# Attention with sink heads, then a soft mixture of experts: one weight loaded in 18 pieces, a fixed order behind the last load, a re-drawn plan

## The chip, the cores and the metric

The kernel runs on one core of a Trainium2 chip. A core has TensorE (PE, matmuls; its weight loads are shown as PEld), VectorE (DVE), ScalarE (ACT), GpSimd (POOL) and SyncE (SP), each with its own instruction queue, and 16 DMA engines that all queues share. The metric is the device time of one execution in microseconds (us), the median of several runs.

## What is computed

```
q, k, v: 4 batches, 8 heads, 768 positions, 64 per head (float32)
scores = q k^T / 8, causal; a head that is not a "retrieval" head sees only
         the first 4 positions and the last 64
x      = softmax(scores) v, as a matrix of 3072 rows by 512
logits = x phi                       (phi: 512 x 32 = 8 experts x 4 slots)
slots  = softmax over the rows(logits)^T x           (32 x 512)
out_e  = relu(slots_e w1[e]) w2[e]   (w1: 512 x 1024, w2: 1024 x 512, 8 experts)
result = softmax over the slots(logits) out          (3072 x 512)
```

All inputs are float32 in memory: q, k and v together 18.9 MB, w1 and w2 together 33.6 MB. The loads convert them to bfloat16 on the way.

## The kernel before

**Stages.** The attention runs in 16 steps (`p = 4*b + n`: batch b, head pair n). Per batch, q, k and v are loaded raw (`load_raw`, 768 KB each as it lands), turned by TensorE (`Tq`, `Tk`, `Tv`, line 513), and copied out (`Eq`, `Ek`, `Ev`). Per step there are score matmuls (`QK`, line 538), exponentials on ScalarE (`EX`, line 609), masks on VectorE (`MK`, line 555), the product with v (`PV`, line 669), the norm (`NM`, line 683) and the turning of the result (`XT`, `XE`). Per batch, the logits and the slots are gathered (`LG`, `EL`, `DS`, `SA`, `TE`, `EE`). When the last batch is through, the experts run for all 32 slots: `SI`, `H` (first matmul), `HR` (relu), `TH`/`HE` (turning), `W2.0` to `W2.7` (second matmul, line 882).

**The loads.** 29 large loads are issued from GpSimd by `dma`/`load_w`/`load_raw` (line 281): q, k, v of four batches, the eight first weights w0 to w7 and the eight second weights w8 to w15. 11 buffers of 8 KB per partition (`slot`, class S8) hold raw inputs and weights in turn; the last weights go into memory that attention has left (`late_mem`). The last weight, w15, comes in two loads: w15a holds 5 of its 8 parts (`FL = 5`), w15b the other 3. w5 is one load of 2 MB (1 MB as it lands), 128 rows of 4096 values.

**Behind the last load.** `SOa` (line 891, ScalarE) scales what the weights up to w15a have made. The first 512 result rows (group 0, four tiles r = 0 to 3, the first of them in two halves) do not wait for the rest: `OM.0.r` multiplies them with SOa's result, and `OG.0.r` adds the part of w15b by three matmuls with operands `gT`, prepared beforehand by `GP.x` (line 911) and `GE.x`. Meanwhile `W2b` (three matmuls with w15b's parts) and `SOb` (line 891, ScalarE: "the late scaling") make the complete slot output, from which all further tiles are multiplied (`OM.1.0.0` and on, line 935). Each tile is scaled and copied out (`OE`, lines 951 on ScalarE and 953 on VectorE) and stored by SyncE (`ST`, line 964) in ten stores.

**The order.** The order of every engine's instructions is not written out: `Plan.run` simulates the engines with estimated durations, picks at each step the operation that can start first (within 0.12 us, by the lowest key), and the kernel emits the operations in that order. Each engine then runs its queue strictly in order, with semaphore waits. `SHIFT` adds an offset to the key of named operations, `ALT` fixes the engine of others; both are long tables of drawn numbers. `FETCH` is the estimated time that TensorE needs for the next block of 128 instructions. In `dma`, an operation `issue` costs 0.62 on GpSimd in the plan, and its `emit` calls one `dma_start`. The plan has buffers for PSUM: classes SC (2), TR (2) and PV (1).

**Zeros.** Where the plan sees TensorE idle in the tail up to the last weight, matmuls with zeros (line 1034) fill the time.

Of the kernel before, what the change touches and what calls it, by code (L numbers as in the profile page):

```python
# [15 lines left out]
ACT = mybir.ActivationFunctionType  # L16
# [3 lines left out]


SHIFT = {
    "phi cast": 1.5, "phi": 6.5, "Tv0.1": 3.5, "Tv0.3": 8, "Tq1.0": -0.5, "Tq1.2": 2, "Tk1.1": 8, "Tk1.2": -1,
    "Tk1.3": 4, "Tv1.1": 3, "Ek2.1": -3.5, "Tk2.2": 3.5, "Tk2.3": 2, "Tv2.0": 8, "Eq3.0": 1, "Tq3.1": 5.5,
    "Tq3.3": 1, "Tk3.0": 8, "Tk3.2": -3.5, "Tv3.0": 3.5, "Ev3.1": -7, "QK.1.3": 3, "QK.1.4": 3, "MK.1.2": 4.5,
    "QK.2.0": -2, "QK.2.1": 2.5, "QK.2.2": 8, "QK.2.3": -5.5, "QK.2.4": -2.5, "VB.3": -6.5, "QK.3.2": 7.5,
    "MK.3.1": 8, "QK.3.4": 4.5, "QX.0.2": 8, "MK.4.0": -3, "QK.4.2": 4.5, "EX.4.3": -6.5, "QK.4.4": 4.5,
    "QK.5.0": -2.5, "QK.5.1": -1, "QK.5.2": 1.5, "QK.5.4": -1.5, "QK.6.3": -2, "QK.6.4": 3, "MK.6.2": 2.5,
    "EX.7.0": -7.5, "EX.7.3": -7, "MK.7.1": -4, "QK.8.0": -8, "QK.8.2": -7.5, "QK.8.4": -8, "VB.9": -5,
    "QK.9.2": -2, "MK.9.2": 4.5, "V2.10": 4, "QK.10.3": 4, "MK.10.1": 5, "V2.11": -1, "QK.11.0": 1.5,  # L30
    "QK.11.1": 1.5, "QK.11.3": 8, "MK.11.2": -7, "QX.2.0": -4.5, "V2.12": 8, "QK.12.0": -6, "QK.12.1": 3,
    "MK.12.1": 4, "QK.13.2": 0.5, "QK.13.3": -2.5, "MK.13.1": -4.5, "V2.14": -2, "QK.14.2": -1.5, "MK.14.2": -8,
    "QK.15.0": -2.5, "XE.0": 2.5, "PV.2.0": 6.5, "PV.3.0": 4.5, "PV.4.3": 8, "PV.5.0": 4, "PV.7.4": -2,
    "PV.7.5": -3.5, "DS.1": 3, "PV.8.0": 4.5, "PV.8.5": 4, "XT.9": 7.5, "XT.10": 7, "XT.12": 5, "PV.13.1": 5,
    "PV.13.5": 7.5, "XT.13": 8, "PV.15.0": -2, "H.1.0": -8,
}
ALT = {
    "Ev0.3": 0, "Eq1.1": 0, "Ek1.2": 1, "Ek1.3": 0, "Ev1.2": 0, "Eq2.1": 0, "Eq2.3": 0, "Ek2.0": 0, "Ek3.1": 1,
    "Ek3.3": 0, "Ev3.0": 0, "VB.7": 0, "VB.13": 0, "EE.1": 0, "EE.2": 0, "XE.14": 0, "HR.1.0": 1,
}  # L40


# [12 lines left out]
class Plan:  # L55
# [3 lines left out]
    OVERLAP = {"ACT": 0.10, "DVE": 0.085, "GEN": 1.45}  # L59
    SWITCH, BONUS, ACTPEN = 0.13, 4.0, 0.4  # L60

    CHUNK, FIRST, FETCH = 128, 97, 5.5

    def __init__(self, classes):
        self.ops, self.free = [], {c: [(0.0, s) for s in range(n)] for c, n in classes.items()}
# [107 lines left out]
def kernel(  # L173
# [13 lines left out]
    nc = tc.nc  # L187
    P = 128
    B, H, S, D = q.shape
# [26 lines left out]
    phi = sb.tile([P, 4, NS], BF16, name="phi")  # L216
# [29 lines left out]
    scb = [ps.tile([P, 2, 512], F32, name=f"sc{i}") for i in range(2)]  # L246
    trb = [ps.tile([P, 512], F32, name=f"tr{i}") for i in range(2)]
    pvb = ps.tile([P, 2, 512], F32, name="pv")

    def tr_bf(s, n):  # L250
# [9 lines left out]
    NGT, FL = 4, 5  # L260
    gT = mk[:, 3200:3200 + 128 * NGT * (8 - FL)].rearrange("p (f c) -> p f c", c=128 * NGT)
    slot_out_a = mk[:, 4736:5248]
    hg = mk[96:128, 5248:5248 + 128 * (8 - FL)].rearrange("p (f c) -> p f c", c=128)
# [3 lines left out]
    pl = Plan({"S8": 11, "QT": 2, "KT": 2, "VT": 1, "VB": 2, "VF": 3, "PT": 2, "PTX": 2, "XB": 2,  # L267
               "XT": 1, "SC": 2, "TR": 2, "PV": 1})
# [3 lines left out]
    def copy(o, dst, src):  # L272
        if o.eng == "ACT":
            nc.scalar.copy(dst, src)
        else:
            nc.vector.tensor_copy(dst, src)  # L276


    def dma(name, key, nbytes, ndesc, buf, dst, src, deps=()):
        iss = pl.op("issue " + name, {"POOL": 0.62}, key, deps=deps, acq=[buf] if buf else [], lead=1.3,  # L280
                    emit=lambda o: nc.gpsimd.dma_start(dst(), src))  # L281
        issues.append(iss)
        gen = pl.op("gen " + name, {"GEN": 1.45}, key, deps=[iss])
        return pl.op("land " + name, {"DMA": dma_us(nbytes, ndesc)}, key, deps=[gen], lead=3.3)
# [22 lines left out]
    wland = [None] * NW  # L307
    late_mem, last_lands = {}, []

    def w_view(i):  # L310
        m = late_mem[i]() if i in late_mem else slots[wbuf[i].slot][:, :]
        return m.rearrange("p (a f) -> p a f", a=4 if i < NE else 8)

    def load_w(i, key, deps=()):
        if i < NE:
            src = moe_w1[i].rearrange("(di do) f -> di do f", do=4)
        else:
            src = moe_w2[i - NE].rearrange("(fi fo) d -> fi fo d", fo=8)
            if i == NW - 1:
                for k, (f0, f1) in enumerate(((0, FL), (FL, 8))):  # L320
                    last_lands.append(dma(f"w15{'ab'[k]}", key + 0.1 * k, (f1 - f0) << 18, 128, None,
                                          lambda f0=f0, f1=f1: w_view(i)[:, f0:f1, :], src[:, f0:f1, :], deps=deps))
                wland[i] = last_lands[0]
                return
        wland[i] = dma(f"w{i}", key, 2 << 20, 128, None if i in late_mem else wbuf[i],
                       lambda: w_view(i), src, deps=deps)


    def tables(o):
# [232 lines left out]
    for b in range(B):  # L562
        for n in range(4):
            p = 4 * b + n
# [79 lines left out]
    for b in range(B):  # L644
        for n in range(4):
            p = 4 * b + n
# [242 lines left out]
    def emit_so(o, d=None):  # L889
        if o.eng == "ACT":  # L890
            nc.scalar.activation(d, pvb[:, 0, :], ACT.Copy, scale=rcs[:, 0:1])
        else:
# [1 line left out]

    so_a = pl.op("SOa", {"ACT": 0.69, "DVE": 0.74}, kt + 20, deps=[w2o[-1], o_rc], need=[so],
                 emit=lambda o: emit_so(o, slot_out_a))
    w2b = pl.op("W2b", {"PE": 0.3}, kt + 25.25, n=8 - FL, deps=[so_a, last_lands[1]], need=[so],
                emit=lambda o: emit_w2(o, fos=tuple(range(FL, 8))))
    so_b = pl.op("SOb", {"ACT": 0.69}, kt + 29.0, deps=[w2b], rel=[so], emit=lambda o: emit_so(o, slot_out))

# [4 lines left out]
    o_hg = pl.op("HG", {"DVE": 0.4}, kt + 8, deps=hse[1] + [o_rc], emit=emit_hg)  # L905
    ge = []
    for x in range(8 - FL):
        gb = Buf("TR")

        def emit_gp(o, x=x, gb=gb):  # L910
            nc.tensor.matmul(trb[gb.slot][:, 0:128 * NGT].rearrange("p (r c) -> p r c", r=NGT), hg[:, x, :],
                             expT[96:128, 0:NGT, 0:128], start=True, stop=True, tile_position=(96, 0))

        a = pl.op(f"GP.{x}", {"PE": 0.25}, kt + 8, n=1, deps=[o_hg] + [eto[b] for b in range(B)], acq=[gb], emit=emit_gp)
        ge.append(pl.op(f"GE.{x}", {"DVE": 0.62, "ACT": 0.69}, kt + 8, deps=[a], rel=[gb],
                        emit=lambda o, x=x, gb=gb: copy(o, gT[:, x, :], trb[gb.slot][:, 0:128 * NGT])))


    def ot_view(gi):
# [5 lines left out]
    for m, (gi, r, d0, d1) in enumerate(parts):  # L925
        c = ["SC", "TR", "SC", "TR"][m] if m < 4 else pat[(m - 4) % 5]
        bf = Buf(c)

        def bank(bf=bf, c=c, w=d1 - d0):
            return (trb[bf.slot] if c == "TR" else scb[bf.slot][:, 0, :] if c == "SC" else pvb[:, 0, :])[:, 0:w]  # L930

        early = gi == 0 and r < NGT

        def emit_om(o, gi=gi, r=r, d0=d0, d1=d1, bank=bank, early=early):
            nc.tensor.matmul(bank(), out_lhs(gi, r), (slot_out_a if early else slot_out)[:, d0:d1], start=True, stop=not early)

        def emit_og(o, r=r, d0=d0, d1=d1, bank=bank):
            for x in range(8 - FL):
                nc.tensor.matmul(bank(), gT[:, x, 128 * r:128 * (r + 1)], w_view(NW - 1)[:, FL + x, d0:d1],
                                 start=False, stop=(x == 7 - FL))  # L940

        a = pl.op(f"OM.{gi}.{r}.{d0}", {"PE": 0.22 * (d1 - d0) / 512}, kt + 24 + m, n=1,
                  deps=[so_a] if early else [so_b], acq=[bf], emit=emit_om)
        if early:
            a = pl.op(f"OG.{gi}.{r}.{d0}", {"PE": 0.22 * (8 - FL) * (d1 - d0) / 512}, kt + 29 + 0.1 * m, n=8 - FL,
                      deps=[a, last_lands[1]] + ge, need=[bf], emit=emit_og)

        def emit_oe(o, gi=gi, r=r, d0=d0, d1=d1, bank=bank):
            d, sc_ = ot_view(gi)[:, r, d0:d1], rrow[:, 4 * gi + r:4 * gi + r + 1]
            if o.eng == "ACT":  # L950
                nc.scalar.activation(d, bank(), ACT.Copy, scale=sc_)
            else:
                nc.vector.tensor_scalar(d, bank(), sc_, None, op0=ALU.mult)  # L953

        w = (d1 - d0) / 512
        oe.setdefault((gi, r), []).append(
            pl.op(f"OE.{gi}.{r}.{d0}", {e_: u for e_, u in (("ACT", 0.22 + 0.47 * w), ("DVE", 0.21 + 0.54 * w))
                                        if not early or e_ == ("ACT", "DVE", "DVE", "DVE", "ACT")[m]}, kt + 30 + m, deps=[a, o_rw],
                  rel=[bf], emit=emit_oe))
    store_parts = [(0, r, r + 1) for r in range(4)] + [(1, 0, 2), (1, 2, 4)] + [(gi, 0, 4) for gi in range(2, 6)]  # L960
    for gi, r0, r1 in store_parts:
        def emit_st(o, gi=gi, r0=r0, r1=r1):
            dst = out[512 * gi:512 * (gi + 1), :].rearrange("(p r) d -> p r d", r=4)
            nc.sync.dma_start(dst[:, r0:r1, :], ot_view(gi)[:, r0:r1, :])

        pl.op(f"ST.{gi}.{r0}", {"SP": 0.7}, kt + 40 + 4 * gi + r0, deps=[x for r in range(r0, r1) for x in oe[gi, r]],
              emit=emit_st)

    order = pl.run()
# [107 lines left out]
```

## Time and profile before

| | us |
|---|---|
| median of 3 runs | 154.38 (152.85, 154.87, 154.38) |
| profiled execution | 152.3 |
| its span, first to last instruction | 150.5 |
| granted TensorE clock, mean over the span | 0.978 |

| engine | busy us | share of span |
|---|---|---|
| PE | 130.1 | 86% |
| DVE | 117.0 | 78% |
| ACT | 106.1 | 71% |
| POOL | 18.6 | 12% |

The durations that follow come from that one execution, counted from the span's start. The loads from GpSimd carry 26.22 MB as it lands (52.49 MB read from memory), the stores 6.29 MB.

Some single events that the text refers to: q3 is issued at 38.05 and its sixteen completion records (one for each DMA engine) lie at 69.72 to 72.46; those of w4 end at 62.94, those of w5 lie at 66.04 to 68.91, those of w15a end at 127.79, those of w15b lie at 125.80 to 129.75. The first store is issued at 131.32, the last at 140.26.

In the profile's timeline a line has start, duration, engine, line, operation, output and input, count, and in brackets the idle time of the engine before it with what ended it. In the chain of waits a line has start, duration, engine, output and line. The slices cut the span into 40 equal parts of 3.76 us; a digit is the busy share in tenths.

### The profile page before, as it was taken

The numbers are of one execution on the slowest core, as the hardware profiler recorded it, in microseconds if no ns is written. First come the engines' busy times: TensorE is split into PE (matmuls) and PEld (weight loads), VectorE is DVE, ScalarE is ACT, GpSimd is POOL, SyncE is SP. The second block draws the span as 40 slices with busy tenths as digits, with TensorE's granted clock in tenths as the row PEclk, the third lists the DMA queues.
The fourth block names the chain that finished last, engine by engine and source line by source line (L and its number), as shares of the span: only waits on it lengthen the run. The fifth ranks groups of instructions, "written<-read, shape, count | busy, mean of one in ns | idle before, by whom it ended". The sixth has DMA issues, their size and how long they took to land.

```text
span 150.5 us, 5245 instructions
## 1 busy us (share of the span) xinstructions
PE 130.1 (86%) x2328; PEld 83.4 (55%) x2328; DVE 117.0 (78%) x243; ACT 106.1 (71%) x126; POOL 18.6 (12%) x38
## 2 busy tenths in 40 slices
PE   6999998999989999888999998998899899798000
PEld 2465565676766677584677766765674444332000
DVE  3889489998789999877999898999976970289200
ACT  3083899889899998788999998999903340379100
POOL 6922111110110001101001202010300000000000
PEclk9999999999999999999999999999999999999965
DMA  3999999999999999999999999999999997079993
GB/s 42 198 212 219 219 209 212 218 223 211 214 211 214 222 216 218 211 212 211 217 221 217 218 216 213 218 213 216 216 218 216 216 205 151 7 255 404 429 422 163
DMA packets 6552, 32.90 MB, mean 219 GB/s; under 512 B 642, under 2 KB 770, under 8 KB 4098
## 3 DMA queue, kind: packets, MB, share of 16 engines
q0 software_dynamic: 4944, 26.22, 85.3%
q1 hardware_dynamic: 1440, 6.29, 10.4%
q8 instruction: 18, 0.29, 0.7%
q10 hardware_dynamic: 146, 0.07, 0.2%
q14 instruction: 4, 0.03, 0.1%
HBM read 52.49 MB, written 6.29 MB: 391 GB/s over the span
## 4 chain that ended last, share of the span: by engine, by line
PE 56%; DVE 18%; ACT 13%; issue 5%; DVEq 0%; ACTq 0%
ACT pt L609 12%; PE pv L669 10%; PE sc L538 10%; PE tr L513 8%; PE pv L1034 6%; PE pv L416 3%; PE tr L695 3%; PE pv L882 3%; DVE pt L555 3%; PE tr L572 3%; DVE slot L953 2%; DVE rcs L811 2%; DVE vx L276 2%; DVE xv L683 2%; DVE qk L276 2%
## 5 line engine op out<-in xcount | busy, mean ns | idle before, releaser
L609 ACT ACTIVATE pt<-sc 128x1024 bf16<-128x1024 f32 x80 | 76.7, 1035 | 5.3 <-PE sc L538 4.4
L538 PE MATMUL sc<-qk 64*128 64x512 bf16 (+3 forms) x256 | 30.7, 307 | 1.5 <-ACT pt L609 0.8
L555 DVE TENSOR_TENSOR pt<-pt,msk 128x1024 bf16<-128x1024 bf16 (+1 forms) x48 | 30.4, 640 | 0.7 <-ACT pt L609 0.6
L669 PE MATMUL pv<-vx,pt 128*128 128x65 bf16 x352 | 26.5, 193 | 0.6 <-issue 0.6
L669 PEld LDWEIGHTS <-pt 128*128 128x128 bf16 x640 | 23.7, 97 | 5.7 <-issue 4.4
L513 PEld LDWEIGHTS <-slot 96*64 96x64 bf16 x768 | 18.6, 110 | 7.9 <-issue 6.5
L513 PE MATMUL tr<-ident,slot 96*64 96x96 bf16 x704 | 21.3, 208 | 0.9 <-issue 0.7
L669 PE MATMUL pv<-vf,pt 128*128 128x65 bf16 x288 | 21.2, 194 | 0.0
L683 DVE TENSOR_TENSOR xv<-pv,rs 128x768 bf16<-128x768 f32 x16 | 15.3, 958 | 0.6
L538 PEld LDWEIGHTS <-qk 64*128 64x128 bf16 x256 | 10.5, 94 | 8.6 <-issue 2.8
L276 DVE COPY qk<-tr 128x768 bf16<-128x768 bf16 x23 | 12.3, 550 | 0.0
L281 POOL DMA_DIRECT2D slot<-in_moe_w_dram x11 | 6.1, 559 | 38.2 <-PE tr L513 27.8
L1034 PE MATMUL pv<-zero 128*128 128x512 bf16 (+1 forms) x43 | 10.2, 373 | 0.0
L953 DVE TENSOR_SCALAR slot<-tr,rrow 128x512 f32<-128x512 f32 (+1 forms) x6 | 4.0, 701 | 7.4 <-issue 6.8
L572 PE MATMUL tr<-ident,xv 128*128 128x128 bf16 x96 | 8.1, 220 | 1.7 <-issue 1.7
L276 DVE COPY xv<-tr 128x768 bf16<-128x768 bf16 x14 | 7.4, 551 | 2.6 <-PE tr L513 2.4
L276 DVE COPY vx<-tr 128x768 bf16<-128x768 bf16 x14 | 7.7, 553 | 2.1 <-PE tr L572 2.1
L695 PE MATMUL tr<-ident,xv 128*128 128x128 bf16 x96 | 8.0, 219 | 0.8 <-DVE xv L683 0.5
L276 DVE COPY xT<-tr 128x768 bf16<-128x768 bf16 x14 | 7.7, 552 | 0.9 <-PE tr L695 0.8
L572 PEld LDWEIGHTS <-xv 128*128 128x128 bf16 x96 | 5.6, 97 | 4.1 <-issue 3.7
L1034 PEld LDWEIGHTS <-zero 128*128 128x128 bf16 x59 | 4.9, 97 | 5.3 <-issue 1.1
L695 PEld LDWEIGHTS <-xv 128*128 128x128 bf16 x96 | 5.7, 97 | 3.1 <-issue 1.5
(122 smaller groups left out, 159.3 us busy)
## 6 DMA issues: line engine op xcount, KB each, us to landing
slot<-in_moe_w_dram POOLq DMA_DIRECT2D x11, 1024.0 KB, 23.9
out_dram<-slot SPq DMA_DIRECT2D x4, 1024.0 KB, 7.6
slot<-in_q_dram POOLq DMA_DIRECT2D x4, 768.0 KB, 26.8
slot<-in_k_dram POOLq DMA_DIRECT2D x4, 768.0 KB, 27.9
slot<-in_v_dram POOLq DMA_DIRECT2D x4, 768.0 KB, 23.2
qk<-in_moe_w_dram POOLq DMA_DIRECT2D x1, 1024.0 KB, 18.7
vx<-in_moe_w_dram POOLq DMA_DIRECT2D x1, 1024.0 KB, 21.5
xv<-in_moe_w_dram POOLq DMA_DIRECT2D x1, 1024.0 KB, 20.0
```

The lines of the kernel that those rows point to most:

```text
L276: nc.vector.tensor_copy(dst, src)
L281: emit=lambda o: nc.gpsimd.dma_start(dst(), src))
L513: nc.tensor.transpose(t[64 * i:64 * (i + 1), :, s, :], rv[:, i, 8 * c + s, :], ident[0:96, 0:96])
L538: nc.tensor.matmul(scb[sc.slot][:, i, c:c + 128 * nb], kk, qq.rearrange("p b c -> p (b c)"), start=True, stop=True)
L555: nc.vector.tensor_tensor(pw, pw, mw, op=ALU.mult)
L572: nc.tensor.transpose(t[:, 128 * j:128 * (j + 1)], vT[:, 6 * n + j, :], ident)
L609: nc.scalar.activation(pTs[PTb[b, n].slot][:, :, 512 * g:512 * (g + 1)], scb[sc.slot], ACT.Exp, scale=scale)
L669: nc.tensor.matmul(pvb[:, h, 65 * i:65 * (i + 1)], lt, rhs, start=(j == 0), stop=(j == i))
L683: nc.vector.tensor_tensor(xo, pvw[:, :, :, 0:64], r.rearrange("p i (j o) -> p i j o", o=1).to_broadcast([P, 2, 6, 64]), op=ALU.mult)
L695: nc.tensor.transpose(t[:, 128 * i:128 * (i + 1)], xv[:, i, 128 * n:128 * (n + 1)], ident)
L953: nc.vector.tensor_scalar(d, bank(), sc_, None, op0=ALU.mult)
L1034: nc.tensor.matmul(bank[:, c0:c0 + w], zero[:, 0:128], zero[:, 0:w], start=(c0 == 0), stop=True, skip_group_check=True)
```

## The change

Five things change:

1. `dma` takes a list `cuts`, and issues one `dma_start` for each cut. w5 alone gets such a list, `UNEVEN`, of 18: rows 0 to 111 whole; rows 112 to 127 from value 1024 on; and for n = 0 to 7 the 128 values from 128 n on, once for rows 112 to 126 - n and once for rows 127 - n to 127. The plan's cost of the issue is 0.62 for each piece.
2. `SHIFT` and `ALT` are replaced by other drawn numbers, for all stages; `FETCH` is 6.2 instead of 5.5.
3. Behind w15b, TensorE's order is written out by added dependences: OM of the tiles (0,0) in two halves, (0,1), (0,2), then OG of the same, then W2b, then OM and OG of (0,3), then OM.1.0.0. The plan's cost and key of W2b change.
4. The engines of the first five OE are ACT, DVE, DVE, ACT, DVE instead of ACT, DVE, DVE, DVE, ACT. The third GP/GE pair uses a bank of class SC instead of TR.
5. A store's cost on SyncE in the plan is 0.4 instead of 0.7.

```diff
 SHIFT = {
-    "phi cast": 1.5, "phi": 6.5, "Tv0.1": 3.5, "Tv0.3": 8, "Tq1.0": -0.5, "Tq1.2": 2, "Tk1.1": 8, "Tk1.2": -1,
...
+    "phi cast": 7.5, "P2": 5, "Tk0.2": -2.5, "Tk0.3": -1.5, "Eq1.3": 2, "Ek1.2": 3.5, "Tk1.3": 3.5, "Tv1.1": 8,
...
-    CHUNK, FIRST, FETCH = 128, 97, 5.5
+    CHUNK, FIRST, FETCH = 128, 97, 6.2
...
-    def dma(name, key, nbytes, ndesc, buf, dst, src, deps=()):
-        iss = pl.op("issue " + name, {"POOL": 0.62}, key, deps=deps, acq=[buf] if buf else [], lead=1.3,
-                    emit=lambda o: nc.gpsimd.dma_start(dst(), src))
+    def dma(name, key, nbytes, ndesc, buf, dst, src, deps=(), cuts=()):
+        def emit(o):
+            d = dst()
+            for r, c in cuts or [(slice(None), None)]:
+                if c is None:
+                    nc.gpsimd.dma_start(d[r], src[r])
+                else:
+                    nc.gpsimd.dma_start(d[r].rearrange("p a f -> p (a f)")[:, c],
+                                        src[r].rearrange("p a f -> p (a f)")[:, c])
+
+        iss = pl.op("issue " + name, {"POOL": 0.62 * max(1, len(cuts))}, key, deps=deps, acq=[buf] if buf else [], lead=1.3,
+                    emit=emit)
...
+    UNEVEN = [(slice(0, 112), None), (slice(112, 128), slice(1024, 4096))]
+    for n in range(8):
+        cut = slice(128 * n, 128 * (n + 1))
+        UNEVEN += [(slice(112, 127 - n), cut), (slice(127 - n, 128), cut)]
...
-                       lambda: w_view(i), src, deps=deps)
+                       lambda: w_view(i), src, deps=deps, cuts=UNEVEN if i == 5 else ())
...
-    w2b = pl.op("W2b", {"PE": 0.3}, kt + 25.25, n=8 - FL, deps=[so_a, last_lands[1]], need=[so],
+    w2b = pl.op("W2b", {"PE": 0.55}, kt + 29.0, n=8 - FL, deps=[so_a, last_lands[1]], need=[so],
...
-        gb = Buf("TR")
+        gb = Buf("TR" if x < 2 else "SC")
...
-                                        if not early or e_ == ("ACT", "DVE", "DVE", "DVE", "ACT")[m]}, kt + 30 + m, deps=[a, o_rw],
+                                        if not early or e_ == ("ACT", "DVE", "DVE", "ACT", "DVE")[m]}, kt + 30 + m, deps=[a, o_rw],
...
+    tail = {o.name: o for o in pl.ops}
+    seq = ["OM.0.0.0", "OM.0.0.256", "OM.0.1.0", "OM.0.2.0", "OG.0.0.0", "OG.0.0.256", "OG.0.1.0", "OG.0.2.0", "W2b",
+           "OM.0.3.0", "OG.0.3.0", "OM.1.0.0"]
+    for x, y in zip(seq[:-1], seq[1:]):
+        tail[y].deps.append(tail[x])
+        tail[y].ndep += 1
+        tail[x].succ.append(tail[y])
...
-        pl.op(f"ST.{gi}.{r0}", {"SP": 0.7}, kt + 40 + 4 * gi + r0, deps=[x for r in range(r0, r1) for x in oe[gi, r]],
+        pl.op(f"ST.{gi}.{r0}", {"SP": 0.4}, kt + 40 + 4 * gi + r0, deps=[x for r in range(r0, r1) for x in oe[gi, r]],
```

## The prediction

> **What bounds the kernel now.** I read the page's slices first.
>
> ```profile
> PE   6999998999989999888999998998899899798000
> DMA  3999999999999999999999999999999997079993
> GB/s 42 198 212 219 219 209 212 218 223 211 214 211 214 222 216 218 211 212 211 217 221 217 218 216 213 218 213 216 216 218 216 216 205 151 7 255 404 429 422 163
> ```
>
> The DMA row is at its ceiling from the second slice to the 33rd: the loads run without a hole from 2.80 us (first packet) to 129.75 us, then there is a hole of one slice, then the stores. Next the chain of waits, at the end of the loads.
>
> ```profile
> 123.41 3.21 PE pv L882 x56
> 126.61 1.24 PE pv L1034 x6
> 127.86 0.59 PE pv L882 x5
> 128.47 0.70 ACT msk L891
> ```
>
> The second expert matmul has eaten seven weights by 126.61, fills the time with zeros (L1034) and goes on at 127.86, when w15a has landed: so the loads set the end, and compute is ahead of them by 1.24 us. What follows w15b's landing at 129.75 is a fixed tail of 20.75 us to the span's end at 150.5; the profiled execution took 152.3, so 1.8 lie outside the span. The runs have their median at 154.38 (152.85 to 154.87): the sum below is made on 152.3, and 2.1 us are added for the median.
>
> Third, GpSimd's timeline, the queue that issues every large load.
>
> ```profile
> 7.06 0.58 POOL L281 DMA_DIRECT2D slot<-in_moe_w_dram  x1
> 8.45 0.65 POOL L281 DMA_DIRECT2D slot<-in_moe_w_dram  x1 [0.80 <-DMA slot<-in_q_dram]
> 12.12 0.76 POOL L281 DMA_DIRECT2D slot<-in_q_dram  x1 [3.02 <-DMA slot<-in_k_dram]
> 16.73 0.64 POOL L281 DMA_DIRECT2D slot<-in_k_dram  x1 [3.84 <-DMA slot<-in_v_dram]
> ...
> 33.09 0.53 POOL L281 DMA_DIRECT2D slot<-in_moe_w_dram  x1 [3.33 <-PE tr L513]
> 38.05 0.65 POOL L281 DMA_DIRECT2D slot<-in_q_dram  x1 [4.43 <-DMA slot<-in_moe_w_dram]
> 42.64 0.64 POOL L281 DMA_DIRECT2D slot<-in_k_dram  x1 [3.94 <-PE pv L669]
> ```
>
> The ninth load (w2, at 8.45) goes into a slot nobody has used, and still waits for q0, the first; the tenth waits for k0, the second; the eleventh for v0, the third. The completions fall on eight semaphores in turn, and each issue waits for the load eight before it on the same one (w1, the eighth, lands at 37.47, and q3, the sixteenth, goes out at 38.05). So at most eight GpSimd loads are in flight, whatever their size. With loads of 0.75 to 1 MB that is some 30 us of queue: w5, out at 33.09, lands at 68.91.
>
> **The change, part by part.**
>
> *The triangle.* w5 becomes 18 loads: one of 112 rows, one of 16 rows by 3072 values, and 16 of 128 values by 1 to 15 rows. Call them w5.0 to w5.17; they take 18 places in the eight-deep window, and q3, k3, v3 and all later weights stand behind them on GpSimd. w5.0 to w5.7 replace old loads as these land (the last place comes free with w4's landing, 62.94). w5.8 must wait for w5.0 itself, w5.9 for w5.1, and so on; q3 comes after w5.17. So when w5.0 has landed, nothing of size is queued, and the DMA engines run dry until q3.
>
> When: w5's sixteen completion records lie at 66.04 to 68.91. A weight's packet of 8192 bytes takes 0.62 us in the packet records, and w5.0 has one row less per engine, so its last engine is done at 68.91 - 0.62 = 68.3; call it 68.4 at GpSimd. Then ten small issues. One issue takes 0.53 with 128 rows and 0.64 with 192: by a straight line a piece of at most 15 rows takes 0.34, by the nearest row 0.53. I take 0.40, nearer the line since 15 rows are far below 128: 10 x 0.40 = 4.0, q3 goes out at 72.4 (71.8 to 73.7). Completions do not delay it more: q3 waits for w5.10, issued at about 69.2, and a 64 KB load on an idle queue (phf) landed in 1.8: 71.0. From issue to first packet the first load took 2.80 - 1.31 = 1.5: data again at 73.9 (73.3 to 75.2).
>
> What the hole costs at the end: the engine that ends w5 last (68.91) has 129.69 - 68.91 = 60.8 to go, the next (67.83) at most 129.75 - 67.83 = 61.9. After the hole all engines start together at 73.9, so the last ends at 134.7 to 135.8 in place of 129.75: **+5.0 to +6.1, taken as +5.5**; with the bounds of the restart +4.3 to +7.4.
>
> The packets themselves: by 0.324 us for 4096 bytes and 0.624 for 8192, 256 bytes take 0.043; 16 of them and 17 more completion packets of 0.022 are 1.1 us at most on one engine. They run inside the hole: nothing, as long as there is a hole; without it, up to +0.4 on all engines for the completions.
>
> *Compute behind the hole.* q3's transposes stand on TensorE at 75.07; q3 needed 3.6 from w5's end to its own, so it lands at 77.5. TensorE stands 2.5 us there, 5 if the new order puts them right behind the old landing (72.46). The cover is 1.24 + 5.5 = 6.7 us ahead of w15a, so nothing; if the cover is gone, the excess is paid in full.
>
> *The new table and the longer fetch* (6.2 for 5.5) add no instruction; they change the order on all engines. As the loads are the bound, a better order gains nothing before w15a and a worse one costs nothing up to 6.7 - 5 = 1.7 us. Bounds 0 to +1; taken as 0. The third GP in the other bank lies at 122.5, ahead of the wait for w15a: 0, by the same cover.
>
> *The order behind w15b.* Before, W2b goes at 131.46 and OG.0.2.0 at 131.79 (0.65); now OG.0.2.0 goes first, and W2b some 0.33 later. OE.0.2.0 moves from VectorE to ScalarE, where SOb (0.69) ran 131.91 to 132.60.
>
> ```profile
> 130.38 0.47 ACT L951 ACTIVATE slot<-sc,rrow 128x256 f32<-128x256 f32 x1 [1.23 <-PE sc L939]
> 131.91 0.69 ACT L891 ACTIVATE msk<-pv,rcs 128x512 bf16<-128x512 f32 x1 [1.05 <-PE pv L882]
> 133.30 0.69 ACT L951 ACTIVATE slot<-sc,rrow 128x512 f32<-128x512 f32 x1 [0.70 <-PE sc L939]
> ```
>
> If OE.0.2.0 is queued ahead of SOb, SOb ends 0.7 later, and OM.1.0.0 and the full rate of tiles behind it start up to 0.7 later; against that the third store goes 0.7 earlier (132.7 for 133.43). The stores are short of tiles only until 135.5 (228 to 257 GB/s in the two stretches before, 428 after 137.5), so both signs are possible: -0.5 to +0.7, taken as +0.2. SP's 0.4 for 0.7 is a planning cost; the ten stores keep their order.
>
> **Sum:** 152.3 + 5.5 + 0 + 0.2 = 158.0 on the profiled execution, 160.1 as a median.
>
> **Rivals.**
>
> *A, the pieces are cheap and the hole is short (same or just slower).* If an issue cost 0.2 and the first packet followed after 1.0, q3's data would start at 68.4 + 2.0 + 1.0 = 71.4, and the end would move by +2.5 to +3.5, say +2.9: 155.2 (as a median 157.3). Against it: no issue in the trace is under 0.53. Chance 0.10.
>
> *B, the triangle evens out the engines (faster).* w15b's sixteen completions lie at 125.80 to 129.75, eight before 127.1 and eight after 128.0, mean 127.3; the late ones are as late as the trace's 18 instruction fetch packets (16 KB, 0.95 us each) make them if they fall on half of the engines. If small loads went more to the early engines, an even finish would bring the landing forward by at most 2.4, and with the tail's best 0.7 that is 149.2 (151.3). It decides only if q3 goes out before w5.0 lands, some 68 us, and the rows of 8.45 to 16.73 speak against that; also the pieces can shift only 16 x 0.043 = 0.7 us between the first and the last engine, which leaves 151.5 (153.6). Chance 0.07, of that 0.04 for over 2%. [...]
>
> *C, compute takes over the end (much slower).* TensorE stands for q3, and then the replanned order is out of step with late k3 and v3. It decides if the delay exceeds 6.7 us. The granted clock stays at 1.00 for 5 us after the last matmul (139.04 to 143.99) and is 0.50 after that, so a wait of over 5 us would also halve the clock for a while. Price: 2 to 4 on top, 160 to 162 (162 to 164). Chance 0.11. [...]
>
> **How the numbers follow.** The forecast has 0.72. 160 us is its median. The range runs from 155.8 (the profiled execution's 152.3 + 4.3 - 0.5 = 156.1, and a little lower for A) to 163.5 (the median's 154.4 + 7.4 + 0.7 = 162.5, and part of C). The median's spread over three runs is 1.3%, and 2% (3.1 us) is about what a measurement of this kernel can tell from no change. Over 157.5 lie all of the forecast (its lowest median is 154.4 + 4.3 - 0.5 = 158.2) and C: 0.83; within 2% A and the smaller part of B, 0.13; faster 0.04.
>
> **What would show it.** In the changed trace: GpSimd's issues of w5 come in two groups, eight up to some 63 us and ten packed together from about 68; q3 is issued behind them at 72 to 74; the DMA share has a hole of 3 to 7 us around 70; w15b lands at 134 to 137; W2b stands behind OG.0.2.0, and the tail is 20 to 21.5 us long. If q3 goes out before 67 us or the hole is missing, the main step is wrong; if the hole is there and the end has not moved, compute and not the loads was the bound.

## The result, and the profile after

The changed kernel takes 160.48 us (median of 4 runs, 160.39 to 160.59), the kernel before 154.57 (152.85 to 154.87). The ratio is 1.0491, 95% interval 1.0443 to 1.0539: slower by some 7.5 us. The two medians lie only 5.9 apart, because the ratio leaves slow runs out, and three of these four runs of the kernel before were slower than most of its later ones, for a reason that the record does not show. In the four later sessions the kernel before took 152.31 to 152.98, so 7.5 is the better figure for what the change does. The profiled execution of the changed kernel took 160.39, span 158.6, against 152.3 and 150.5.

The page's slices of the changed kernel (3.97 us each):

```profile
PE   7999999989989899883079988999989999599000
...
POOL 6911111111111110169300102110130000000000
PEclk9999999999999999999759999999999999999965
DMA  3999999999999999801999999999999999459994
GB/s 44 202 213 217 215 211 215 218 227 207 210 217 219 212 225 205 165 10 10 171 215 227 207 223 207 223 211 221 207 225 217 213 215 208 80 198 389 414 415 171
```

Where the DMA row of before was full from the second slice to the 33rd, there is now a hole around the 18th, two slices at 10 GB/s. GpSimd is busy there, and a slice later TensorE stands still and its clock falls. GpSimd's timeline says what it was doing (start, duration, line, operation, output and input, count, idle time before):

```profile
35.12 0.55 POOL L286 DMA_DIRECT2D slot<-in_moe_w_dram  x1 [5.03 <-PE tr L530]
37.84 0.51 POOL L288 DMA_DIRECT2D slot<-in_moe_w_dram  x1 [2.17 <-DMA slot<-in_moe_w_dram]
42.71 0.53 POOL L288 DMA_DIRECT2D slot<-in_moe_w_dram  x1 [4.36 <-DMA slot<-in_moe_w_dram]
46.35 0.50 POOL L288 DMA_DIRECT2D slot<-in_moe_w_dram  x1 [3.12 <-DMA slot<-in_q_dram]
...
63.47 0.50 POOL L288 DMA_DIRECT2D slot<-in_moe_w_dram  x1 [4.37 <-DMA slot<-in_moe_w_dram]
68.93 4.93 POOL L288 DMA_DIRECT2D slot<-in_moe_w_dram  x10 [4.96 <-DMA slot<-in_moe_w_dram]
73.85 0.68 POOL L286 DMA_DIRECT2D slot<-in_q_dram  x1
74.51 0.66 POOL L286 DMA_DIRECT2D slot<-in_k_dram  x1
```

The piece of 112 rows, w5.0, goes out at 35.12, and the next seven pieces one by one, each when one of the seven older loads has landed; the last of the eight places is taken at 63.47. Then GpSimd waits 4.96 us for w5.0 itself (its last completion record is at 68.65), sends ten pieces in 4.93 us, and only then q3, at 73.85 instead of 38.05. The chain of waits of the whole execution runs through exactly these lines:

```profile
35.12 33.53 DMA slot<-in_moe_w_dram
68.93 3.85 POOL slot L288 x8
72.86 0.47 POOL slot L288
73.35 0.50 POOL slot L288
73.85 6.54 DMA slot<-in_q_dram
...
117.97 17.74 DMA qk<-in_moe_w_dram
135.74 0.61 PE pv L899 x5
136.37 0.70 ACT msk L908
```

In the chain of before there was no GpSimd at all (and no load either, since the zero matmuls fill TensorE's wait for the last weight). At its other end, w15a ends at 135.70 (127.79 before) and w15b at 136.07 to 137.67 (125.80 to 129.75). What follows w15b is 158.6 - 137.67 = 20.9 us, against 20.75. The hole also set the DMA engines level: w15b's sixteen completions lie 1.6 us apart instead of 3.95, so the first comes 10.3 us later than before and the last only 7.9.

### The profile page after: what moved, and what is told of

It reads as the page before. It is cut to its first block, busy times and chain, and to the rows that moved or that the text cites. A ratio compares the mean times of both kernels' runs of the same rounds, so it can differ in the third digit from the quotient of the medians.

```text
span 158.6 us, 5249 instructions
## 1 busy us (share of the span) xinstructions
PE 129.3 (82%) x2321; PEld 83.1 (52%) x2321; DVE 112.8 (71%) x236; ACT 111.6 (70%) x133; POOL 27.0 (17%) x55
## 4 chain that ended last, share of the span: by engine, by line
DMA 36%; PE 28%; ACT 19%; POOL 3%; issue 3%; DVE 3%; ACTq 0%
DMA slot<-in_moe_w_dram 21%; ACT pt L626 14%; DMA qk<-in_moe_w_dram 11%; PE pv L686 5%; PE sc L555 5%; PE pv L1060 5%; PE tr L530 4%; DMA slot<-in_q_dram 4%; PE pv L433 3%; ACT slot L969 3%; POOL slot L288 3%; DVE xv L700 1%; PE sc L530 1%; PE tr L589 1%; ACT msk L908 1%
## 5 line engine op out<-in xcount | busy, mean ns | idle before, releaser
L626 ACT ACTIVATE pt<-sc 128x1024 bf16<-128x1024 f32 x80 | 77.6, 1046 | 4.0 <-PE sc L555 3.8
L555 PE MATMUL sc<-qk 64*128 64x512 bf16 (+3 forms) x256 | 31.7, 312 | 5.5 <-ACT pt L626 4.9
L572 DVE TENSOR_TENSOR pt<-pt,msk 128x1024 bf16<-128x1024 bf16 (+1 forms) x48 | 29.8, 641 | 0.7 <-ACT pt L626 0.5
L686 PEld LDWEIGHTS <-pt 128*128 128x128 bf16 x640 | 23.3, 97 | 5.4 <-issue 4.0
L686 PE MATMUL pv<-vx,pt 128*128 128x65 bf16 x352 | 25.6, 193 | 0.2 <-DVE xv L700 0.2
L278 DVE COPY qk<-tr 128x768 bf16<-128x768 bf16 x21 | 11.2, 550 | 8.5 <-PE tr L530 8.5
L288 POOL DMA_DIRECT2D slot<-in_moe_w_dram x17 | 8.5, 504 | 29.7 <-DMA slot<-in_moe_w_dram 20.2
L286 POOL DMA_DIRECT2D slot<-in_moe_w_dram x11 | 6.1, 559 | 35.9 <-PE tr L530 17.9
L650 ACT ACTIVATE vx<-sc 128x1024 bf16<-128x1024 f32 (+1 forms) x5 | 4.4, 875 | 8.8 <-PE sc L555 8.8
L1060 PE MATMUL pv<-zero 128*128 128x512 bf16 (+1 forms) x36 | 8.3, 367 | 0.0
L605 DVE TENSOR_TENSOR vf<-vx,fm 128x528 bf16<-128x528 bf16 x16 | 6.9, 429 | 0.2
L712 PEld LDWEIGHTS <-xv 128*128 128x128 bf16 x96 | 5.7, 97 | 2.4 <-issue 1.1
```

What stands on the lines that cost most here:

```text
L288: nc.gpsimd.dma_start(d[r].rearrange("p a f -> p (a f)")[:, c], src[r].rearrange("p a f -> p (a f)")[:, c])
L555: nc.tensor.matmul(scb[sc.slot][:, i, c:c + 128 * nb], kk, qq.rearrange("p b c -> p (b c)"), start=True, stop=True)
L572: nc.vector.tensor_tensor(pw, pw, mw, op=ALU.mult)
L605: nc.vector.tensor_tensor(vfs[VFb[p].slot], vv, fm[:, n], op=ALU.mult)
L626: nc.scalar.activation(pTs[PTb[b, n].slot][:, :, 512 * g:512 * (g + 1)], scb[sc.slot], ACT.Exp, scale=scale)
L686: nc.tensor.matmul(pvb[:, h, 65 * i:65 * (i + 1)], lt, rhs, start=(j == 0), stop=(j == i))
```

## The experiments

Times are medians; "ratio" is against runs of the kernel before on the same chip, with its 95% interval. The first four ran beside 152.66 us of before, the next four beside 152.98, the three `sb` kernels beside 152.49, the last beside 152.31.

**The triangle alone and all but the triangle.** In `one_load` the changed kernel loads w5 whole; in `tri_only` the kernel of before gets the 18 pieces. The plans keep their costs, so each engine's order stays that of its parent.

```diff
 one_load, from the changed kernel
-        iss = pl.op("issue " + name, {"POOL": 0.62 * max(1, len(cuts))}, ...
+        iss = pl.op("issue " + name, {"POOL": 0.62 * (18 if name == "w5" else 1)}, ...
-                       lambda: w_view(i), src, deps=deps, cuts=UNEVEN if i == 5 else ())
+                       lambda: w_view(i), src, deps=deps, cuts=())
 tri_only, from the kernel before: dma() with cuts, UNEVEN, and
-                       lambda: w_view(i), src, deps=deps)
+                       lambda: w_view(i), src, deps=deps, cuts=UNEVEN if i == 5 else ())
```

> The changed kernel with w5 in one load again; the plan still counts 18 issues for it, so that every engine's order is that of the changed kernel. Theory (eight loads in flight, so 18 pieces in a row drain the queue): the hole near 70 us is gone, the loads end 6 to 8 us earlier, the time is 153.5 to 155.5. Rival (the new plan and the new order behind w15b cost the time, the hole only hides it): 159 to 161.

> The kernel of before with nothing but the 18 pieces of w5; its plan counts one issue, so that every engine's order is that of before. Theory: the hole appears, 159 to 161.5. Rival (plan and order): 154 to 155.5.

`tri_only`: 159.82 us, ratio 1.0458 (1.0413 to 1.0504). `one_load`: 155.80, ratio 1.0196 (1.0154 to 1.0238). By itself the triangle costs as much as the whole change (the two intervals overlap), with the same lines as in the changed kernel:

```profile
63.48 0.50 POOL L286 DMA_DIRECT2D slot<-in_moe_w_dram  x1 [4.39 <-DMA slot<-in_moe_w_dram]
69.15 4.93 POOL L286 DMA_DIRECT2D slot<-in_moe_w_dram  x10 [5.17 <-DMA slot<-in_moe_w_dram]
74.07 0.68 POOL L284 DMA_DIRECT2D slot<-in_q_dram  x1
```

Its last load ends at 137.68, the changed kernel's at 137.67. But `one_load` is a surprise: without the hole its loads end at 130.34, much as before, and it is still some 3 us over the kernel before, more than the theory had. Its tail takes 153.6 - 130.34 = 23.3 us. This is taken up below.

**How many pieces.** `seven` and `eleven` are the changed kernel with two and four pairs of the triangle instead of eight; what the other pairs held is one piece of 16 rows.

```diff
 seven (eleven: slice(512, 1024) and range(4))
     UNEVEN = [(slice(0, 112), None), (slice(112, 128), slice(1024, 4096))]
-    for n in range(8):
+    UNEVEN.append((slice(112, 128), slice(256, 1024)))
+    for n in range(2):
```

> The changed kernel with w5 in 7 pieces in place of 18 (112 rows; 16 rows by 3072; 16 rows by 768; two pairs of the triangle), orders as in the changed kernel. Theory: q3 is the eighth load behind w4, so it goes out when w4 lands, near 63 us, and lies queued when w5 is done: no hole, the time of the one-load kernel to within 0.4 us. Rival (a price per piece: issue, completions, small packets): 7/18 of the loss, some 2.3 us over the one-load kernel.

> The changed kernel with w5 in 11 pieces, orders as in the changed kernel. Theory: three pieces in place of ten are issued after w5's first piece has landed (68.7), 0.49 us each, so q3 goes out 3.4 us earlier than in the changed kernel, at 70.4: 156.5 to 157.7, some 3.4 us under the changed kernel. Rival (a price per piece): 11/18 of the loss, some 2.3 us under the changed kernel.

`eleven`: 156.81 us (156.66 to 156.92), ratio 1.0276 (1.0250 to 1.0302), 3.7 under the changed kernel. `seven`: 155.05 (153.80 to 156.84), ratio 1.0134 (1.0069 to 1.0199), 0.75 under `one_load`, not within the 0.4 expected, but not dearer either. Its runs differ by more than that among themselves, and with the granted clock: 0.968 in the one of 153.80, 0.949 in the one of 156.84 (`one_load`: 0.948 to 0.958). Why is taken up with the clock below. GpSimd in `eleven`, then in `seven`:

```profile
68.88 1.48 POOL L288 DMA_DIRECT2D slot<-in_moe_w_dram  x3 [5.03 <-DMA slot<-in_moe_w_dram]
70.36 0.68 POOL L286 DMA_DIRECT2D slot<-in_q_dram  x1
71.02 0.66 POOL L286 DMA_DIRECT2D slot<-in_k_dram  x1
```

```profile
63.89 0.67 POOL L286 DMA_DIRECT2D slot<-in_q_dram  x1 [4.78 <-PE sc L556]
69.56 0.64 POOL L286 DMA_DIRECT2D slot<-in_k_dram  x1 [5.00 <-PE tr L590]
```

With three pieces behind the landing instead of ten, q3 goes out 3.49 us earlier and w15b ends 3.70 earlier (133.97). With seven in all, q3 takes the last of the eight places at 63.89 and lies queued when w5 is through: there is no hole, and the loads end at 130.89 (`one_load`: 130.34). A price per piece would have given 2.3 us more for `seven` than for `one_load`, and only 2.3 less for `eleven` than for the changed kernel. It is the window of eight that costs.

**The 3 us of `one_load`.** The stretches of `one_load` (length, busy time and count for PE, PEld, DVE, ACT and POOL, then the granted clock, the DMA share and GB/s):

```profile
124.87:128.28 3.41, 2.01 (x24) 0.54 (x13) 1.29 (x2) 0.59 (x1) 0.00 (x0) 1.00 0.65 128
128.28:135.10 6.82, 6.04 (x21) 2.44 (x21) 1.23 (x2) 1.84 (x4) 0.00 (x0) 0.50 0.17 62
```

TensorE's clock is halved from 128.28 to 135.10, while w15b lands and behind it. The new plan puts the three GP matmuls into the gap before W2.7 (in the kernel before they stood at 121.53 to 123.1, ahead of the second expert matmul) and so emits no zero matmuls there, where the kernel before had six; TensorE stands 1.40 us for w15a. In `one_load` the gap looks like this:

```profile
125.51 0.60 PE L929 MATMUL tr<-expT,msk 32*128 32x512 bf16 x2
125.95 0.37 PE L929 MATMUL sc<-expT,msk 32*128 32x512 bf16 x1
127.72 0.59 PE L899 MATMUL pv<-qk,xT 128*32 128x512 bf16 x5 [1.40 <-DMA qk<-in_moe_w_dram]
```

`zeros` is `one_load` with six put back.

```diff
     for o in order:
+        before["W2.7"] = (6, 0, pvb[:, 1, :], 0)     (once, ahead of the loop)
         if o.name in before:
```

> The one-load kernel with six zero matmuls before W2.7, where the kernel of before has six and the changed plan has none. Theory (the one-load kernel's tail of 23.3 us, 2.5 more than before, comes from TensorE's clock, which was 0.50 from 128.3 to 135.1 after TensorE had stood 1.4 us for w15a): the clock stays at 1.00 through the tail, the tail is 20.5 to 21.2 us, the time 152.5 to 153.7. Rival (the new order behind w15b is slower by itself): 155 to 156 as the one-load kernel.

153.01 us (152.79 to 154.03), ratio 1.0026 (0.9999 to 1.0053). The same stretch of `zeros`:

```profile
124.87:128.28 3.41, 3.25 (x33) 1.03 (x22) 1.29 (x2) 0.59 (x1) 0.00 (x0) 1.00 0.63 125
```

The clock now holds to 142.87 and the tail takes 150.7 - 130.23 = 20.5 us. Against the kernel before, 3.0 us (1.96%) have become 0.4 (0.26%, an interval that just reaches 0), so the zeros account for some 2.6. For the new order behind w15b itself next to nothing is left.

**The table and the tail alone**, each put into the kernel before: `table_only` takes `SHIFT`, `ALT` and `FETCH`, `tail_only` all that stands behind `SOa` in the diff.

> The kernel of before with the new tables and the longer fetch alone. Theory (the loads are the bound, the order in front of w15a costs only what it does to the clock): the loads end within 0.8 us of before, and the time is that of before to within 0.6 us if the zeros before W2.7 are still there, 2 to 3 us more if they are gone. Rival (the new order makes the loads or the experts late): the loads end over 1 us later than before.

> The kernel of before with the written-out order behind w15b, the engines of the first five OE, the third GP's bank and the two plan costs alone. Theory: -0.5 to +0.7 us against before, the zeros before W2.7 unchanged. Rival (the tail's change is where the 3 us of the one-load kernel come from): 2 to 3 us over before.

`tail_only`: 152.76 us, ratio 1.0008 (0.9980 to 1.0036): no cost that shows. `table_only`: 152.82, ratio 1.0019 (0.9974 to 1.0065), but in two groups: seven runs of 152.35 to 153.30 with a mean granted clock of 0.965 to 0.978, three of 154.31 to 154.56 with 0.961 to 0.962. Its profiled execution is one of the three, and shows two zero matmuls where before has six, and the clock:

```profile
126.89:130.30 3.41, 1.45 (x10) 0.65 (x10) 0.69 (x1) 0.69 (x1) 0.00 (x0) 1.00 0.23 46
130.30:133.72 3.42, 3.36 (x13) 1.39 (x12) 1.09 (x2) 0.47 (x1) 0.00 (x0) 0.50 0.11 44
```

So with the table alone, TensorE is filled so thinly before w15a (1.45 us busy of 3.41 here) that its clock holds in some executions and not in others; the loads end at 130.32, 0.57 later than before. Neither part loses all six zeros; table and tail together did. The table moves the GP matmuls into the gap; with it alone the third GP goes to a bank of class TR and stands at 126.57, 0.6 us behind the end of the second, which leaves room for two zeros. The tail gives the third GP a bank of class SC, and in `one_load` it follows the second at once.

**The same pieces, spread.** `spread` is `zeros` with all 18 pieces, but only two stand at w5; the rest follow in twos behind the next eight loads. `sb` does the same to the kernel before; `sb_wide` has pieces of 256 values instead of 128; `sb_half` cuts each pair into two times 8 rows.

```diff
 spread, sb (in dma's emit)
+            parts = [(d, src, r, c) for r, c in cuts or [(slice(None), None)]]
+            later.extend(parts[2:])
+            now = parts[:2] + ([] if cuts else [later.pop(0) for _ in range(min(2, len(later)))])
-            for r, c in cuts or [(slice(None), None)]:
+            for d_, s_, r, c in now:
 sb_wide
-    UNEVEN = [(slice(0, 112), None), (slice(112, 128), slice(1024, 4096))]
+    UNEVEN = [(slice(0, 112), None), (slice(112, 128), slice(2048, 4096))]
-        cut = slice(128 * n, 128 * (n + 1))
+        cut = slice(256 * n, 256 * (n + 1))
 sb_half
-        UNEVEN += [(slice(112, 127 - n), cut), (slice(127 - n, 128), cut)]
+        UNEVEN += [(slice(112, 120), cut), (slice(120, 128), cut)]
```

> The kernel 'zeros' with all 18 pieces of w5 again, but only the first two where w5 stands; the 16 small ones follow two at a time behind each of the next eight loads. Theory (a run of small loads drains the eight places, their number does not): no hole, the time of 'zeros' to within 0.6 us. Rival 1 (a price per piece): 4 to 5 us over 'zeros'. Rival 2 (the triangle evens out the engines): w15b's completions lie closer together than in the one-load kernel (4.45 us) and the time is 0.3 us or more under 'zeros'.

> The kernel of before, its tables and its tail untouched, with w5's 18 pieces spread: two where w5 stands, two small ones behind each of the next eight loads. Theory (spread pieces cost the loads some 0.4 us on the mean of the engines and take 0.5 us off the last engine): w15b's completions are 3.3 to 3.7 us apart instead of 3.95, no hole, -0.5 to 0 us against before. Rival (no gain is left, the two cancel): 0 to +0.4.

> As 'sb', with pieces twice as wide (256 values, so that half of the 16 rows goes into the triangle). If the triangle takes from the late engines what it gives to the early ones, the effect grows with the bytes: completions 3.0 to 3.5 us apart, -0.8 to -0.1 us against before. If the pieces fall evenly on all engines: 3.9 to 4.5 us apart, and no gain over 'sb'.

> As 'sb', with each of the eight pairs cut into two times 8 rows, where the triangle has 15 - n and 1 + n. If a small load starts on the first engine, eight engines get all 16 pieces (16 x 0.04 = 0.6 us and the bytes) and eight get none, so completions move by 0.6 us between the halves. If small loads go round the engines, every engine gets 8 and the completions stay 3.9 to 4.5 us apart. Time within 0.6 us of before in both cases.

> The kernel of before once more, for the size of chance in two readings. If w15b's sixteen completions lie 3.8 us or more apart again (3.95 in the first trace), the 3.5 to 3.7 us of the three spread kernels are an effect of the pieces; if they lie 3.7 or less apart, they are within chance. The time is 152 to 153.5 with the clock at 0.967 or more, 154 to 155.8 with a clock of 0.962 or less.

GpSimd in `spread`, around the place of the old hole:

```profile
63.23 0.51 POOL L291 DMA_DIRECT2D slot<-in_moe_w_dram  x1 [4.50 <-DMA slot<-in_moe_w_dram]
68.95 0.65 POOL L289 DMA_DIRECT2D slot<-in_v_dram  x1 [5.21 <-PE tr L715]
69.59 0.50 POOL L291 DMA_DIRECT2D slot<-in_moe_w_dram  x1
72.41 0.50 POOL L291 DMA_DIRECT2D slot<-in_moe_w_dram  x1 [2.32 <-DMA slot<-in_moe_w_dram]
72.93 0.57 POOL L289 DMA_DIRECT2D slot<-in_moe_w_dram  x1
```

| kernel | median us | ratio (interval) | w15b's completions, first to last | mean of the 16 |
|---|---|---|---|---|
| before | | | 125.80 to 129.75 (3.95) | 127.47 |
| before_again | 152.43 | 0.9997 (0.9978 to 1.0017) | 126.01 to 130.10 (4.09) | 127.50 |
| zeros | 153.01 | 1.0026 (0.9999 to 1.0053) | 125.76 to 130.23 (4.47) | 127.47 |
| spread | 152.55 | 1.0002 (0.9981 to 1.0023) | 126.29 to 129.76 (3.48) | 127.84 |
| sb | 152.14 | 0.9988 (0.9974 to 1.0002) | 126.45 to 130.00 (3.55) | 127.94 |
| sb_wide | 151.90 | 0.9976 (0.9959 to 0.9993) | 126.14 to 129.74 (3.61) | 127.80 |
| sb_half | 151.98 | 0.9998 (0.9971 to 1.0025) | 126.17 to 129.85 (3.68) | 127.76 |

The same 18 pieces that cost some 7 us in a row cost nothing that shows when two at a time stand behind a large load: no hole. They bring the sixteen completions 0.3 to 1.0 us closer together, mostly by making the early engines later (the mean rises by 0.3 to 0.5). Of the two readings set out for `sb_wide`, and of the two for `sb_half`, none came as written: twice the bytes did not bring the completions closer (3.61; 3.0 to 3.5 expected), and halves did much the same as the triangle (3.68), neither moving them by 0.6 nor leaving them at 3.9 and more. In the six traces with w5 in one load (the first three of the table, `one_load`, `table_only` and `tail_only`) they lie 3.90 to 4.47 apart, in the four with spread pieces 3.48 to 3.68, in `seven` 2.82. So pieces do something small here, but it is not shown that the triangle's shape does it, nor which engine a piece lands on. `sb_wide` is the only version whose interval lies below the kernel before, by 0.24% (0.07 to 0.41%): the best kernel of the study, by less than half a microsecond. With this many versions tried, one such interval can also be chance.

## Why the prediction was right, and where two terms met by chance

160.0 was forecast and 160.48 measured, and the mechanism is the one forecast: pieces that fill the eight places, a hole in the loads, and an end that moves with the loads. That the number came within 0.5 us is luck, since an error in the hole and one in the median met with opposite signs. The steps:

| step | forecast | measured |
|---|---|---|
| w5.0 landed, GpSimd goes on | 68.4 | 68.93 |
| ten small issues | 10 x 0.40 = 4.0 (0.34 to 0.53 each) | 4.92, 0.49 each |
| q3 goes out | 72.4 | 73.85 |
| its first packet | 73.9 | 75.23 |
| from there to w15b's end | 60.8 to 61.9 | 62.44 |
| w15b's end moves by | +5.5 (+4.3 to +7.4) | +7.92 |
| TensorE stands for q3 | 2.5 to 5 | 7.38 |
| tail behind w15b | +0.2 | +0.2 (from 20.75 to 20.9) |
| from the profiled execution to the median | +2.1 | +0.1 |

*The hole* is right in place and cause, and 2.4 us too small: q3's issue at 73.85, the shift of 7.92 and w15b's end at 137.67 all lie beyond the bounds set for them (73.7, 7.4 and 137). 0.9 of this is the price of a small issue: loads of 192 and 128 rows were carried on in a straight line to 0.34, and 0.40 was chosen near it; a piece of 1 to 16 rows costs 0.49 to 0.53, almost as much as one of 128 rows (mostly 0.53 to 0.59). The nearest row would have been the better choice. 0.5 is w5.0's later landing. The remaining 1.1 lies behind the restart: from q3's first packet to w15b's first completion 60.84 us pass, where before 59.76 lay between the first completions of w5 and w15b. The first sixteen of q3's packets took 0.33 to 1.08 us each where 0.324 is usual (the excess of all of q3's is 0.46 us per engine), so the restarted queue did not run at full speed at once; the prediction had it do so. The trace of before had this in it: its first sixteen packets, at 2.80, took 0.36 to 1.43. For the other 0.6 no cause is shown.

*The median.* 2.1 us were added because the profiled execution of before was 2.1 under its median. The changed kernel's profiled execution is at its median, and the runs of before in later sessions were near 152.5. This add-on was wrong, and by chance it made up for most of what the hole lacked. On the profiled executions the forecast was 158.0 and the time 160.39.

*Compute behind the hole* was hidden as forecast, with less to spare. q3 landed at 80.39, not 77.5, and TensorE stood 7.38 us:

```profile
72.44 0.61 PE L757 MATMUL tr<-xv,elg 128*32 128x512 bf16 x6 [0.31 <-DVE pt L572]
80.44 0.85 PE L530 MATMUL tr<-ident,slot 96*64 96x96 bf16 x16 [7.38 <-DMA slot<-in_q_dram]
...
135.74 0.59 PE L899 MATMUL pv<-qk,xT 128*32 128x512 bf16 x5 [0.81 <-DMA qk<-in_moe_w_dram]
```

The clock was at 0.50 from 77.03 to 83.86. Rival C had this, for waits of over 5 us; here the fall came 4.0 us after the last matmul had ended at 73.05. But w15a came 7.91 later too, and at the end TensorE still waits 0.81 us for it. C's price did not fall due; 0.8 us was left of its cover.

*The new table and fetch at nothing* was right for the changed kernel, and for a reason the prediction did not have. By themselves the parts are within 0.2% of before, but together they take the zero matmuls out of the gap before W2.7, and without the hole that costs some 2.6 us (`one_load` against `zeros`, each by its ratio). In the changed kernel's trace the wait for w15a is 0.81 instead of 1.40 us and the clock holds to 152.13, so the loss does not add to the hole's. The costs of the two parts, 7.2 us for the triangle in the kernel before and 3 for the rest without it, are not additive. The prediction looked for the cost of an order in late loads and late experts, not in what the order does to the zeros.

*The tail.* W2b stands behind OG.0.2.0, and ScalarE takes OE.0.2.0 ahead of SOb (line 908 in the changed kernel), as forecast:

```profile
138.29 0.47 ACT L969 ACTIVATE slot<-sc,rrow 128x256 f32<-128x256 f32 x1 [1.23 <-PE sc L957]
...
139.91 0.69 ACT L969 ACTIVATE slot<-tr,rrow 128x512 f32<-128x512 f32 x1 [1.15 <-PE tr L957]
...
140.49 0.68 ACT L908 ACTIVATE msk<-pv,rcs 128x512 bf16<-128x512 f32 x1
```

SOb starts 2.82 us after w15b's end instead of 2.16, the forecast 0.7. The tail is only 0.2 us longer all the same, and `tail_only` measures 1.0008: of the bounds -0.5 and +0.7 neither was met.

*Rival A* (short hole) fell with the price of an issue (0.49 us, not 0.2). *Rival B* (evened engines) was rightly set small and named its own condition: with q3 out before w5.0 lands, as in the spread kernels, there is a gain of at most 0.41%, a fraction of the 3.1 us that it could have had at most. (Two of its figures are off: the mean of the sixteen completions is 127.47 and not 127.3, and the tail's best was set at 0.5 and not 0.7; that makes 2.8 of the 3.1.) Whether small loads go more to the early engines was not shown: no run here tells which engine a piece takes, only that `sb_half` and `sb`, whose pieces have other numbers of rows, behave alike (completions 3.68 and 3.55 us apart). For one piece the prediction's packets were wrong: the one of a single row went out as sixteen packets of 16 bytes (0.022 us each), not as one of 256 (0.040 for those of the other small pieces).

## What to carry to other kernels

Before a load is cut up, count how many loads of that queue can be in flight, here eight: what mattered was not the number of pieces but how many bytes were queued behind them (the same 18 pieces in the kernel before took 159.82 us in a row and 152.14 in twos behind large loads). So small loads go one or two at a time between large ones, or in a row short enough that a large load still gets one of the places while the last large one runs: seven pieces in a row left no hole here (the loads end at 130.89 us), eleven did (133.97). When an order is re-drawn, look at what fills an engine's waits too: work moved into a gap can push out filler that held the clock (here six zero matmuls, some 2.6 us), and that may show only in some executions, or only after another fault is mended. And two runs' difference between a profiled time and a median is no constant to be added to a forecast.

## What the runs showed of the hardware

A small load issued from GpSimd cost 0.49 to 0.53 us of it, whether it had 1 row or 16; one of 128 rows cost mostly 0.53 to 0.59 (once 0.65), one of 192 mostly 0.63 to 0.68.

After a hole of some 6 us, and at the start of the kernel, the DMA engines' first packets took up to three or four times their usual time (1.08 us in the changed kernel's trace and 1.43 in that of before, for 0.324).

TensorE's clock fell not only when it stood: it was halved behind stretches of 3.41 us in which TensorE was busy for 2.01 (`one_load`) and for 1.45 us (`table_only`), and stayed so for 6.82, 3.42 and, behind the changed kernel's hole, 6.83 us: one or two times 3.41. The two stretches were 59% and 43% busy, so TensorE did not have to be idle through a whole one for the clock to fall.

Busy time is not the measure, though. Within each trace the clock changed only at whole multiples of 3.41 us from its first change (in `one_load` at 5.39, 128.28, 135.10 and 145.34; in the changed kernel at 5.35, 77.03, 83.86 and 152.13), and the first change lay at 4.0 to 6.9 us, so the same wait can fall into one stretch of this grid in one execution and be divided over two in the next. Some stretches at full clock, each on its own trace's grid:

| run | stretch | PE busy us | work, in whole matmuls | clock after |
|---|---|---|---|---|
| `table_only` | 126.89 to 130.30 | 1.45 | 4.3 | 0.50 |
| `eleven` | 71.71 to 75.13 | 1.54 | 4.6 | 0.50 |
| `one_load` | 124.87 to 128.28 | 2.01 | 5.2 | 0.50 |
| `sb_wide` | 137.30 to 140.71 | 1.67 | 5.8 | 0.50 |
| `seven` | 125.23 to 128.64 | 2.07 | 5.8 | 1.00 |
| changed kernel | 145.30 to 148.71 | 1.77 | 6.0 | 1.00 |
| changed kernel | 135.06 to 138.47 | 1.95 | 6.8 | 1.00 |
| before | 137.16 to 140.57 | 1.88 | 6.8 | 1.00 |

A whole matmul is counted as one of 512 columns with the shape `128*128` in the trace; a smaller one counts by its columns and by its shape's share of that (`128*32` and `32*128` are a quarter). Some 16 whole ones fit into a stretch: in a row, one starts 0.216 us (median) after the other in the trace of before. By busy time the two groups overlap; by work they do not, in any of the 560 stretches at full clock of the fourteen traces, and the edge is near 5.8. At half the clock, too, a stretch with 5.7 was followed by half and every one with 6.1 or more by full. The ends of matmuls in a trace are modelled: with the columns put at the start of each record the edge at full clock comes out near 5.2, and the order of the two sides stays. This was counted from the traces; no run was built to test it.

It accounts for three things above. `seven` has no zeros either and waits 1.34 us, but in its trace the work came out at the edge, on the side on which the clock held. The changed kernel's wait of 0.81 us is divided at 135.06, and neither part is thin enough. And in the traces of before and of `zeros` no stretch of 3.41 us between 118 and 134 us, wherever the grid lies, holds less than 8.3 and 6.9, so in these two executions no place of the grid would have been thin enough.
